# Attention's value products in four column tiles of 32, and another order of the PSUM banks

## The chip, the cores and the metric

The kernel runs on one core of one Trainium2 chip. The metric is device time in microseconds of one execution. The kernel before was timed three times: median 342.35 us, 340.76 to 344.26. The trace is of one further execution. Engines are named as the profile names them: PE multiplies matrices (PEld is its weight load), DVE and ACT work element by element, POOL here mostly issues small transfers, SP issues the large ones.

## What is computed

Attention with a soft cap, then a gated MLP over the sequence, then a gated convolution MLP (batch 2, 12 heads, 448 positions, head size 64):

```python
scores = scale * np.matmul(q, k.transpose(0, 1, 3, 2))
scores = cap * np.tanh(scores / cap)
attn = np.exp(scores - np.max(scores, axis=-1, keepdims=True))
attn = attn / (np.sum(attn, axis=-1, keepdims=True) + 1e-09)
x = np.matmul(attn, v)                      # 12 heads side by side: 448 x 768
h = gelu(x @ w_in);  u, v = halves of h     # the gated MLP
x = x + (u * (w_sg @ layernorm(v) + b_sg)) @ w_out
h = relu(x @ w2_in)                         # the gated convolution
out = (h * sigmoid(conv3(h))) @ w2_out
```

## The kernel before

**Attention, pair by pair.** Twelve pairs of heads N (batch times six) are worked one after the other, both heads of a pair side by side in the 128 partitions. Each pair has two halves. `scores(N, half)` makes transposed scores into a PSUM tile `sc` of four banks, of which there is one copy: half 0 takes key blocks g = 0 and 1 of both heads, half 1 takes block 2 of both and block 3, where the last 64 keys of one head and of the other lie in one tile. These matmuls use split float32r operands and 64-row tiles. ACT then makes tanh of `sc` into `raw` (line 317) and exp of `raw` (line 318). `sc` is written anew by the next half, so the next scores wait for that tanh. For half 0 DVE adds `raw`'s two blocks into `sm` (line 342).

**The values.** `values(N, half)` multiplies `raw` (moving operand, 448 columns, float32) with V (stationary operand) into the bank `pv`, of which there are two, and then sums the exponentials into the bank `su` (one copy) by matmuls with ones: 224 columns, four column tiles of 32 (lines 363 to 372). A float32 matmul stands in the trace as two weight loads and two matmuls. Before, the value products are in two column tiles of 64, one for each head, for g < 3, and in one matmul over all 128 columns for g = 3. All these matmuls are issued by the helper `ordered` and have line 305.

**Order.** The loop of lines 452 to 486 issues a half of scores and then a half of values, one half behind and from R = 13 two halves behind (LAGS). Matmuls of the next stage (`mo`, FILL) stand between them at five places. An attribute keeps PE's order as written; the orders of the other engines are made by a scheduler when the program is built, and each engine works through its own in order.

**What DVE does meanwhile.** It copies `su` to `se` (line 389), so that the next pair's sums may be written; prepares Q and K of later pairs (lines 92, 95, 262, 263); decodes the weights of the next stage from float64 words (lines 135 to 152); and normalises each two pairs: a small transfer `ss` out of `se`, issued on POOL (line 397), a reciprocal (lines 406, 407), two more transfers, a product (line 423) and a split (line 95). The last pair is normalised by PE (`norm_pe`, line 442: `rp`, in a tile of tag `su`; line 446 reads it).

**The next stage.** `rest()` takes seven banks (pool `ps1`) where attention's banks were. Its first unit in that pool is `v_unit` (lines 603 to 605).

Of the kernel before, what the change touches and what calls it, by code (L numbers as in the profile page):

```python
# [9 lines left out]
F32 = mybir.dt.float32  # L10
# [6 lines left out]
P = 128  # L17
B, H, S, D = 2, 12, 448, 64
# [30 lines left out]
def stages(  # L49
# [23 lines left out]
    def pin(last):  # L73
        return tc.issue_after(last[0].ins) if last[0] is not None else ExitStack()
# [12 lines left out]
    def f(ap):  # L87
        return ap.bitcast(F32)
# [130 lines left out]
    def attention(att, psa):  # L219
# [26 lines left out]
        vf = {}  # L246
# [30 lines left out]
        if WARM:  # L277

            wz = att.tile([P, S], F32R, name="wz")
            V.memset(f(wz), 0.0)  # L280
            wps = psa.tile([P, 512], F32, tag="su", name="wps", bufs=1)[:, :S]
            for i in range(WARM):
                T.matmul(wps, lhsT=wz[:, :P], rhs=wz, start=True, stop=True)
        constants(att)
# [17 lines left out]
        def ordered(*args, **kw):  # L302

            with pin(lastm):
                lastm[0] = T.matmul(*args, **kw)  # L305
# [38 lines left out]
        def values(N, half):  # L344
            if half == 0:
                acc[N] = (
                    psa.tile([P, 512], F32, tag="pv", name="pv", bufs=2)[:, :S],
                    psa.tile([P, 512], F32, tag="su", name="su", bufs=1)[:, : S // 2],
                )
            ps, su = acc[N]  # L350
            raw = raws.pop((N, half))
            for g in range(2 * half, 2 * half + 2):
                if g < 3:
                    for h in range(2):
                        r = slice(h * D, (h + 1) * D)
                        ordered(
                            ps[r], lhsT=vf[N][:, g, r], rhs=raw[:, g % 2 * 2 + h],
                            start=g == 0, stop=False, skip_group_check=True,
                        )
                else:  # L360
                    ordered(ps, lhsT=vf[N][:, 3], rhs=raw[:, 2], start=False, stop=True, skip_group_check=True)

            for g in range(2 * half, 3 * half + 1):
                x = raw if half else held.pop(N)
                for t in range(4):
                    h, c = t // 2, (t % 2) * (S // 2)
                    ordered(
                        su[t * 32 : (t + 1) * 32],
                        lhsT=ones[2 if g < 3 else h],
                        rhs=x[:, h if g < 3 else 2, c : c + S // 2],  # L370
                        start=g == 0, stop=g == 3, tile_position=(0, t * 32), skip_group_check=True,
                    )
            if half:
                del acc[N]
                norm(N, ps, su)
# [76 lines left out]
        for R in range(2 * NN + LAGS[1]):  # L452
            N, half = divmod(R, 2)
# [5 lines left out]
            if R < 2 * NN:  # L459
                if half == 0 and N + 2 < NN:  # L460
                    load(N + 2)
                if R == 1:

                    scores(N, half, lambda: values(0, 0))
                    done += 1
                else:
                    scores(N, half)
                if half == 0 and N + 1 < NN:
                    prep_q(N + 1)
                    prep_k(N + 1)  # L470
# [10 lines left out]
            if R - done >= LAGS[R >= LAGS[2]]:  # L481
                values(*divmod(done, 2))
                done += 1
# [414 lines left out]
```

## Time and profile before

| | us |
|---|---|
| median of three runs | 342.35 |
| the profiled execution, whole | 343.89 |
| its span | 342.10 |
| PE busy in the span | 329.2 (96%) |
| DVE busy | 252.9 (74%) |
| ACT busy | 224.9 (66%) |
| attention, first scores to the first `v_unit` | 7.55 to 127.96 |

The profile is of one execution; times are counted from its span's start. A row of the timeline has start, duration, engine, line, operation, tiles written and read, and a count of the instructions merged into it; what stands in brackets is the engine's idle time before it and what ended that. A matmul's start is recorded, its end is modelled, so distances between starts are what is read.

### The profile page before, as it was taken

The numbers are of one execution on the slowest core, as the hardware profiler recorded it, in microseconds if no ns is written. First come the engines' busy times: TensorE is split into PE (matmuls) and PEld (weight loads), VectorE is DVE, ScalarE is ACT, GpSimd is POOL, SyncE is SP. The second block draws the span as 40 slices with busy tenths as digits, with TensorE's granted clock in tenths as the row PEclk, the third lists the DMA queues.
The fourth block names the chain that finished last, engine by engine and source line by source line (L and its number), as shares of the span: only waits on it lengthen the run. The fifth ranks groups of instructions, "written<-read, shape, count | busy, mean of one in ns | idle before, by whom it ended". The sixth has DMA issues, their size and how long they took to land.

```text
span 342.1 us, 5132 instructions
## 1 busy us (share of the span) xinstructions
PE 329.2 (96%) x1814; PEld 252.2 (74%) x1814; DVE 252.9 (74%) x493; ACT 224.9 (66%) x361; POOL 35.8 (10%) x71
## 2 busy tenths in 40 slices
PE   5999999999999999999999999999999999999992
PEld 4544444544456558898899999999999999999991
DVE  3378878889974477997999779997995999970000
ACT  1689988997897246576875554465884988873110
POOL 3000300311034113121111000000000000000000
PEclk9699999999999999999999999999999999999998
DMA  5859555748122114313123383002284113013111
GB/s 174 243 143 278 178 156 158 216 118 218 47 66 63 44 54 148 93 46 94 62 68 119 107 281 150 0 0 62 63 273 158 33 61 92 3 55 126 64 55 34
DMA packets 18698, 37.67 MB, mean 110 GB/s; under 512 B 3980, under 2 KB 9160, under 8 KB 18664
## 3 DMA queue, kind: packets, MB, share of 16 engines
q1 hardware_dynamic: 16952, 34.41, 32.7%
q0 software_dynamic: 1472, 2.61, 2.9%
q8 instruction: 16, 0.26, 0.4%
q10 hardware_dynamic: 240, 0.23, 0.2%
q14 instruction: 18, 0.15, 0.1%
HBM read 34.41 MB, written 2.79 MB: 109 GB/s over the span
## 4 chain that ended last, share of the span: by engine, by line
PE 79%; DMA 7%; DVE 7%; issue 3%; POOL 1%; ACT 0%; SPq 0%; DVEq 0%; ACTq 0%; POOLq 0%
PE mo L98 18%; PE mo L99 17%; PE mo L100 17%; PE pv L305 6%; PE sc L305 5%; PE mo L603 3%; PE mo L604 3%; PE mo L605 3%; PE mo L305 3%; PE su L305 3%; DMA kr<-in_kT_dram 2%; DMA ss<-se 2%; DMA qr<-in_qT_dram 2%; PE idle L305 1%; DVE Q L263 1%
## 5 line engine op out<-in xcount | busy, mean ns | idle before, releaser
L98 PE MATMUL mo<-X,WI 128*128 128x448 f32 x126 | 46.1, 367 | 0.0
L99 PE MATMUL mo<-X,WI 128*128 128x448 f32 x126 | 45.9, 366 | 0.0
L100 PE MATMUL mo<-X,WI 128*128 128x448 f32 x126 | 45.9, 365 | 0.0
L305 PE MATMUL pv<-raw,V 128*64 128x448 f32 (+1 forms) x168 | 43.7, 561 | 0.0
L305 PE MATMUL sc<-Q,K 64*128 64x448 f32 (+1 forms) x252 | 39.7, 398 | 3.4 <-DVE K L92 2.3
L318 ACT ACTIVATE raw<-raw,one 128x1792 f32<-128x1792 f32 (+3 forms) x26 | 39.1, 1503 | 0.6
L305 PEld LDWEIGHTS sc<-Q,K 64*128 64x128 f32 (+1 forms) x252 | 24.8, 190 | 18.0 <-issue 8.1
L130 ACT ACTIVATE f<-f 128x512 f32<-128x512 f32 (+3 forms) x57 | 30.9, 544 | 10.4 <-DMA f<-in_w_out_dram 6.0
L140 DVE SCALAR_TENSOR_TENSOR f<-f 128x512 uint32<-128x512 uint32 (+3 forms) x57 | 30.7, 547 | 9.2 <-ACT f L133 8.7
L317 ACT ACTIVATE raw<-sc 128x1792 f32<-128x1792 f32 (+1 forms) x22 | 32.5, 1475 | 6.8 <-PE sc L305 5.9
L99 PE MATMUL mo<-HG,W 128*128 128x448 f32 x96 | 34.8, 365 | 0.0
L100 PE MATMUL mo<-HG,W 128*128 128x448 f32 x96 | 34.7, 365 | 0.0
L98 PE MATMUL mo<-HG,W 128*128 128x448 f32 x96 | 34.1, 365 | 0.0
L143 DVE SCALAR_TENSOR_TENSOR f<-f 128x512 uint32<-128x512 uint32 (+3 forms) x57 | 30.9, 548 | 0.2
L305 PEld LDWEIGHTS pv<-raw,V 128*64 128x64 f32 (+1 forms) x168 | 11.8, 143 | 21.4 <-issue 18.6
L98 PEld LDWEIGHTS mo<-X,WI 128*128 128x128 f32 x126 | 23.6, 188 | 2.4 <-DVE u L179 0.4
L99 PEld LDWEIGHTS mo<-X,WI 128*128 128x128 f32 x126 | 23.7, 188 | 2.0
L100 PEld LDWEIGHTS mo<-X,WI 128*128 128x128 f32 x126 | 23.6, 188 | 2.0
L783 ACT ACTIVATE o<-mo 128x448 f32<-128x448 f32 x12 | 6.3, 540 | 25.6 <-PE mo L100 22.5
L133 ACT ACTIVATE f<-f 128x256 uint32<-128x256 uint32 (+2 forms) x44 | 22.6, 514 | 0.0
L99 PEld LDWEIGHTS mo<-HG,W 128*128 128x128 f32 x96 | 18.0, 188 | 1.4
L98 PEld LDWEIGHTS mo<-HG,W 128*128 128x128 f32 x96 | 18.0, 188 | 1.4
(141 smaller groups left out, 653.3 us busy)
## 6 DMA issues: line engine op xcount, KB each, us to landing
f<-in_w_in_dram SPq DMA_DIRECT2D x24, 512.0 KB, 4.9
f<-in_w_out_dram SPq DMA_DIRECT2D x24, 256.0 KB, 4.4
V<-in_vL_dram SPq DMA_DIRECT2D x12, 256.0 KB, 4.2
f<-in_w_out_dram SPq DMA_DIRECT2D x8, 384.0 KB, 3.1
qr<-in_qT_dram SPq DMA_DIRECT2D x24, 112.0 KB, 3.2
out_dram<-o SPq DMA_DIRECT2D x12, 224.0 KB, 1.9
rb<-d POOLq DMA_DIRECT2D x22, 112.0 KB, 3.2
kr<-in_kT_dram SPq DMA_DIRECT2D x11, 112.0 KB, 2.6
```

The costliest lines, as they stand in the source:

```text
L98: matmul(ps, lhsT=whi, rhs=xhi, start=start, stop=False)
L99: matmul(ps, lhsT=whi, rhs=xlo, start=False, stop=False)
L100: matmul(ps, lhsT=wlo, rhs=xhi, start=False, stop=stop)
L130: A.activation(f(h), f(h), AF.Copy, scale=2.0**-112)
L133: A.activation(l, l, AF.Copy, scale=0.93 * 2.0**-29)
L140: V.scalar_tensor_tensor(out=l, in0=h, scalar=3, in1=l, op0=ALU.logical_shift_left, op1=ALU.bitwise_or)
L143: V.scalar_tensor_tensor(out=l, in0=h, scalar=0x80000000, in1=l, op0=ALU.bitwise_and, op1=ALU.bitwise_or)
L305: lastm[0] = T.matmul(*args, **kw)
L317: A.activation(raw[:, t], ps[:, t, :S], AF.Tanh, **sc)
L318: lasta[0] = A.activation(raw[:, t], raw[:, t], AF.Exp, scale=capc)
L603: T.matmul(ps, lhsT=xs(0, k), rhs=WI[1][:, 0, k], start=k == 0, stop=False)
L604: T.matmul(ps, lhsT=xs(0, k), rhs=WI[1][:, 1, k], start=False, stop=False)
```

## The change

In `values` every block g is now done in four column tiles of 32, each with its own weight load and its own position, g = 3 too. The moving operand of a tile is still the 448 columns of its head. And the ten warm-up matmuls at the start, whose output is not used, write a tile of tag `sc` rather than `su`. That tag is then the first to be laid out, so that `sc` lies in banks 1 to 4, `pv` in 5 and 6 and `su` in 7, where it was `su` in 1, `sc` in 2 to 5 and `pv` in 6 and 7; the first tile of `ps1` is in bank 1 both times.

```diff
-            wps = psa.tile([P, 512], F32, tag="su", name="wps", bufs=1)[:, :S]
+            wps = psa.tile([P, 4, 512], F32, tag="sc", name="wps", bufs=1)[:, 0, :S]
...
             for g in range(2 * half, 2 * half + 2):
-                if g < 3:
-                    for h in range(2):
-                        r = slice(h * D, (h + 1) * D)
-                        ordered(
-                            ps[r], lhsT=vf[N][:, g, r], rhs=raw[:, g % 2 * 2 + h],
-                            start=g == 0, stop=False, skip_group_check=True,
-                        )
-                else:
-                    ordered(ps, lhsT=vf[N][:, 3], rhs=raw[:, 2], start=False, stop=True, skip_group_check=True)
+                for t in range(4):
+                    r = slice(t * 32, (t + 1) * 32)
+                    ordered(
+                        ps[r], lhsT=vf[N][:, g, r], rhs=raw[:, g % 2 * 2 + t // 2 if g < 3 else 2],
+                        start=g == 0, stop=g == 3, tile_position=(0, t * 32), skip_group_check=True,
+                    )
```

On PE, in the middle of attention, from the scores of one pair's second half on (`K_87` and `K_88` are the two copies of K, `ones_136` to `ones_138` the three tiles of ones):

```order
 L305 MATMUL sc<-Q,K_88 128x448 x9
-L305 MATMUL pv<-raw,V 64x448 x4
+L305 MATMUL pv<-raw,V 32x448 x8
 L305 MATMUL su<-sm,ones_138 32x224 x4
 L305 MATMUL sc<-Q,K_87 128x448 x12
-L305 MATMUL pv<-raw,V 64x448 x2
-L305 MATMUL pv<-raw,V 128x448
+L305 MATMUL pv<-raw,V 32x448 x8
 L305 MATMUL su<-raw,ones_138 32x224 x4
 L305 MATMUL su<-raw,ones_136 32x224 x2
 L305 MATMUL su<-raw,ones_137 32x224 x2
```

Nothing changes its place; seven value matmuls of a pair became sixteen, and value products and sums have one tile shape.

At attention's end on PE, before, with the semaphores waited for (DVE_49 is counted up by DVE, Activation_49 by ACT):

```order
L442 MATMUL rp<-r,sel 64x224 [waits DVE_49,PE_49,Pool_49]
L442 MATMUL rp<-r,sel 64x224 [waits Pool_49]
L442 MATMUL rp<-r,sel 64x224
L442 MATMUL rp<-r,sel 64x224 [waits Pool_49]
L603 MATMUL mo<-WI_77,X 128x512 [waits DVE_49,Activation_49]
```

And the same place now, where lines are three lower:

```order
L439 MATMUL rp<-r,sel 64x224 [waits DVE_49,PE_49,Pool_49]
L439 MATMUL rp<-r,sel 64x224 [waits Pool_49]
L439 MATMUL rp<-r,sel 64x224
L439 MATMUL rp<-r,sel 64x224 [waits Pool_49]
L600 MATMUL mo<-WI_77,X 128x512 [waits DVE_49,Activation_49]
```

Nothing moved, and the first `v_unit` has the waits that it had: in both programs the value that it waits for on DVE is the one set by the product that reads `rp` (line 446, now 443).

On DVE, from the arrival of `ss` to the next copy of `su`, before (`f` are weight pieces in decoding, `WI` where they go):

```order
L406 TENSOR_SCALAR ss<-ss,one 128x14
L135 TENSOR_SCALAR f_530<-f_530 128x512
L423 TENSOR_TENSOR E<-E,rb 128x896
L263 SCALAR_TENSOR_TENSOR Q<-qr,one,Q 128x448
L143 SCALAR_TENSOR_TENSOR f_452<-f_452 128x512
L407 RECIPROCAL ss<-ss 128x14
L149 CAST WI_76<-f_452 128x512
L152 TENSOR_TENSOR WI_76<-f_452,WI_76 128x512
L389 COPY se<-su 128x224
```

And now:

```order
L403 TENSOR_SCALAR ss<-ss,one 128x14
L135 TENSOR_SCALAR f_566<-f_566 128x512
L420 TENSOR_TENSOR E<-E,rb 128x896
L263 SCALAR_TENSOR_TENSOR Q<-qr,one,Q 128x448
L143 SCALAR_TENSOR_TENSOR f_479<-f_479 128x512
L404 RECIPROCAL ss<-ss 128x14
L149 CAST WI_76<-f_479 128x512
L152 TENSOR_TENSOR WI_76<-f_479,WI_76 128x512
L386 COPY se<-su 128x224
```

The order is the same. Over the part of the program that runs, DVE's order differs in one place only, where a weight split (line 152) and a K cast (line 92) that stood next to each other have changed places; the orders of ACT, POOL and SP are the same.

## Rows read from the trace of the kernel before

**Rows 1.** Page, part 1: busy us, share of the span, instructions.

```profile
PE 329.2 (96%) x1814; PEld 252.2 (74%) x1814; DVE 252.9 (74%) x493; ACT 224.9 (66%) x361; POOL 35.8 (10%) x71
```

**Rows 2.** Timeline, PE: values of pair 3, half 0, up to the next scores.

```profile
41.10 0.60 PE L305 MATMUL pv<-raw,V 128*64 128x448 f32 x2
41.53 0.92 PE L305 MATMUL pv<-raw,V 128*64 128x448 f32 x4
42.28 0.55 PE L305 MATMUL pv<-raw,V 128*64 128x448 f32 x2
42.76 0.40 PE L305 MATMUL su<-sm,ones 128*32 128x224 f32 x4
42.97 0.37 PE L305 MATMUL su<-sm,ones 128*32 128x224 f32 x4
43.27 0.47 PE L305 MATMUL sc<-Q,K 64*128 64x448 f32 x2
```

**Rows 3.** Timeline, PE: values of pair 3, half 1, up to the next scores.

```profile
44.69 0.60 PE L305 MATMUL pv<-raw,V 128*64 128x448 f32 x2
45.12 1.12 PE L305 MATMUL pv<-raw,V 128*64 128x448 f32 x3
45.59 1.02 PE L305 MATMUL pv<-raw,V 128*128 128x448 f32 x2
46.07 0.54 PE L305 MATMUL pv<-raw,V 128*128 128x448 f32 x1
46.54 0.40 PE L305 MATMUL su<-raw,ones 128*32 128x224 f32 x4
47.13 0.37 PE L305 MATMUL su<-raw,ones 128*32 128x224 f32 x4
47.43 0.47 PE L305 MATMUL sc<-Q,K 64*128 64x448 f32 x2
```

**Rows 4.** Groups by shape, weight loads of the sums: busy us, mean ns.

```profile
L305 PEld LDWEIGHTS su<-raw,ones 128*32 128x32 f32 x192 | 5.0, 109 | 9.2 <-issue 7.8
```

**Rows 5.** Busy us in stretches: PE, PEld, DVE, ACT, POOL, clock granted, DMA.

```profile
20.84:47.43 26.59, 26.59 (x201) 11.64 (x199) 21.56 (x44) 23.95 (x22) 3.70 (x6) 1.00 0.64 188
53.15:64.23 11.08, 11.08 (x88) 4.87 (x84) 11.01 (x21) 10.73 (x10) 2.94 (x5) 1.00 0.60 179
69.74:87.79 18.05, 17.16 (x124) 8.18 (x123) 17.98 (x34) 15.56 (x15) 2.96 (x5) 1.00 0.60 159
56.72:80.00 23.28, 22.13 (x161) 10.67 (x160) 20.69 (x39) 22.86 (x21) 6.31 (x11) 1.00 0.68 194
90.09:96.21 6.12, 6.12 (x50) 2.50 (x50) 5.69 (x13) 6.08 (x6) 0.50 (x1) 1.00 0.18 47
```

**Rows 6.** Timeline, DVE: copies of su (pairs 3, 5, 7) and arrivals of ss.

```profile
47.57 0.39 DVE L389 COPY se<-su 128x224 f32<-128x224 f32 x1 [0.90 <-PE su L305]
53.15 0.23 DVE L406 TENSOR_SCALAR ss<-ss,one 128x14 f32<-128x14 f32 x1 [1.25 <-DMA ss<-se]
63.84 0.38 DVE L389 COPY se<-su 128x224 f32<-128x224 f32 x1
69.74 0.23 DVE L406 TENSOR_SCALAR ss<-ss,one 128x14 f32<-128x14 f32 x1 [1.95 <-DMA ss<-se]
87.40 0.39 DVE L389 COPY se<-su 128x224 f32<-128x224 f32 x1
```

**Rows 7.** Timeline, PE: sums of pair 7, and the first v_unit.

```profile
78.49 0.38 PE L305 MATMUL su<-sm,ones 128*32 128x224 f32 x2 [0.83 <-DVE se L389]
127.96 0.47 PE L603 MATMUL mo<-WI,X 128*128 128x512 f32 x1 [0.84 <-DVE E L446]
```

**Rows 8.** Timeline, PE and DVE: scores of pair 10, and attention's last handover.

```profile
96.31 0.48 PE L305 MATMUL sc<-Q,K 64*128 64x448 f32 x2
121.49 0.62 DVE L179 SCALAR_TENSOR_TENSOR u<-g,mo 128x448 f32<-128x448 f32 x1 [0.64 <-ACT g L176]
122.29 0.47 PE L98 MATMUL mo<-X,WI 128*128 128x448 f32 x1
```

## The prediction

> **What bounds the kernel now.** I read the page's busy times first: PE is busy in 96% of the span [rows 1], so at first sight whatever PE saves is saved. Then the timeline of PE through one unit of values, to see where time between two matmul starts is more than streaming. Then the busy times of all engines in stretches of attention, because a mean over the span hides that DVE and ACT are full for a part of it [rows 5]. Last the timeline of DVE, to see what its full stretches hang on [rows 6], and the two places where PE waits for DVE [rows 7].
>
> A wave is what I call the matmuls that start within some 20 ns of each other, in different column tiles. In half 0 a wave of two 64-column tiles comes every 0.375 us: 42.28 less 41.53, over two [rows 2]. The first wave takes 0.43, because its weights are not there yet. From the last value wave to the first sum it is 0.48, so 0.105 beyond a wave. A wave of four 32-column tiles, at half the columns, comes every 0.19 (46.54 to 47.13 less a first wave of 0.21, over two), which is half of 0.375 [rows 2, 3]. The last wave of sums to the next scores takes 0.30, 0.11 beyond a wave. In half 1 the change from 64 to 128 columns costs 0.095 (0.47 for a wave), the second weight load of the 128-column tile 0.105 (0.48), the change from 128 to 32 again 0.095 (0.47) [rows 3]. So each change of the tile's shape costs about 0.1 us of PE, and the wider the tile, the more of its first weight load shows.
>
> The whole of half 0's values takes 43.27 less 41.10, 2.17 us, half 1's 47.43 less 44.69, 2.74 us [rows 2, 3]. There are twelve of each.
>
> **What the change does on PE.** Half 0 and half 1 become alike: four waves of values, then two or four of sums, all in one shape. A wave of values with four tiles of 448 columns is not in the trace. Its bounds: 0.375 (twice the 0.19 of four tiles at 224 columns, and also what two tiles take at 448) and 0.75 (if only two of the four ran together). I take 0.375: the sums are the same instruction, float32, 128 rows, four tiles of 32, and differ in the columns alone. First wave: 0.375 and 0.02, as the sums' first is 0.21 against 0.19. From values to sums: between 0 and the present 0.1 beyond a wave; I take 0, since the sums change their moving operand and their weights from g = 2 to g = 3 without a step (the 0.19 above covers it).
>
> Half 0: 0.40 + 3 x 0.375 + 0.19 + 0.30 = 2.015, so 0.155 less. Half 1: 0.40 + 3 x 0.375 + 3 x 0.19 + 0.30 = 2.395, so 0.345 less. A pair saves 0.50 us of PE, twelve pairs 6.0 us. The additional weight loads (32 instead of 14 records for a pair) lie behind running waves, as the sums' do; if that cover were gone, see the third rival.
>
> **The warm-up's tile.** PE's own order keeps warm-up before scores, so the new wait of the first scores costs nothing. At the end, the first v_unit waits 0.84 us for the product that reads rp [rows 7]. Its tile now lies where scores were, not where rp is, but the built program still has the same two waits there, as the order shows. I cost this at 0; the other end is a gain of 0.84.
>
> **How much of 6.0 us arrives.** PE's saving becomes time only where PE is what is waited for.
>
> Up to 47.4 us it is. From 20.84 to 47.43 PE is never idle, DVE is busy 21.56 of 26.59 us and ACT 23.95 [rows 5]. Shortened by three and a half pairs, the stretch is about 24.8 long, so ACT is nearly full but not over. Pairs 0 to 3 lie here: 4 x 0.50 = 2.0 us.
>
> From 47.57 to 87.79 it is not. The copy of pair 3's sums at 47.57 releases the transfer ss, which lands 5.2 us after the copy's end, at 53.15, and DVE sits behind it in its order. Then DVE is busy 11.01 of 11.08 us up to the end of the copy of pair 5's sums. That releases the next transfer, which lands after 5.5 us, at 69.74. Then DVE is busy 17.98 of 18.05 us up to the end of the copy of pair 7's sums at 87.79 [rows 5, 6]. No matmul stands in this chain of 40.2 us; it moves with its start, by 2.0 us, and is no shorter. PE meets it at sm and at su: it already waits 0.83 at pair 7 [rows 7]. What pairs 4 to 7 save, some 2 us, turns into more waiting at those places. ACT is no better: in 56.72 to 80.00 it is idle for 0.42 us [rows 5].
>
> After 87.84 PE leads again, with half 1 of pair 8 and pairs 9 to 11 still to come. Two more places take some back. The scores of pair 10 start at 96.31, and ACT, full since 90.09, ends the tanh they need at 96.2 [rows 5, 8]; that leaves 0.1 of the 0.345 + 0.155 saved just before, and I count 0.05. Then 0.345, 0.155, 0.345 and 0.155 arrive. Of pair 11's last 0.345, the handover keeps all but some 0.1: the matmuls at 122.29 need u, whose last step ends at 121.49 + 0.62 = 122.11 and hangs on matmuls that stand before that half [rows 8]. Sum: 0.05 + 1.00 + 0.1 = 1.15, in all 2.0 + 1.15 = 3.15, say 3.1 us. What comes after moves as a whole, as PE is its bound (96% [rows 1]).
>
> The profiled execution took 343.89 us around a span of 342.10, so 340.8 by its own time. The median of the runs is 342.35, 0.45% below it; the same 3.1 us puts the prediction at **339.2 us**.
>
> **Rivals.**
>
> *The transfers land sooner.* In the chain, ss is slow (5.2 and 5.5 us) when large loads are under way. If the new alignment shortened it, ACT would be the next bound: 2.0, pair 4's 0.50, ACT's 0.42, then 0.35 of pair 7 and the last 1.15, 4.4 us in all: 338.0. Against it: the loads are issued behind the same DVE work and move along with it. If not even ACT held, all of 6.0 us would arrive: 336.3; ACT's 0.42 us of idle time speaks against that.
>
> *The step from values to sums stays.* If the 0.1 belongs to the change of operands and not to the shape, each unit loses 0.1 + 0.02 of its saving: 0.035 and 0.225, a pair 0.26. Four pairs give 1.05, the end about half of 1.15: 1.6 us, 340.7. Against it: between 64 and 128 columns, within one accumulation, the step is as large [rows 3].
>
> *The weight loads come out of cover, and the kernel is slower.* All four tiles use all 128 rows. If a tile's load had to wait for running matmuls of other tiles, each wave would show at least one load of 0.109 us [rows 4]: 4 x 0.109 x 24 = 10.5 us more, less 6.0: 4.5 us slower, 346.8. It decides from 0.063 us in each wave (6.0 over 96 waves), so from waves of 0.44 us. Against it: the sums' waves come at 0.19 with eight loads in 0.38 us [rows 3]. [...]
>
> *The bank order does what it seems meant for.* If the first v_unit no longer waited for rp's reader, 0.84 more: 338.4. The order's waits speak against it.
>
> *Nothing arrives*: the saving is all taken by waits on exp or sm already before 47 us: 342.3.
>
> **Chances.** Forecast 0.55 (its own range 338.4 to 340.0), transfers sooner 0.15, all of it 0.04, step stays 0.14, loads out of cover 0.05, bank order 0.03, nothing 0.04. The range 336.8 to 341.4 takes in the first, second, fourth and sixth with their spread and leaves out under 0.2. About 1% is what a measurement of this kernel can tell from no change. Below 338.9 us lie the second, third and sixth case, and a third of the forecast's own spread: faster 0.40. Slower is the loads' case: 0.05. The rest, 0.55, is within 1%.
>
> **What would show it.** Value waves 0.375 us apart with four matmuls each, and no step from values to sums, so half 0 at 2.0 and half 1 at 2.4 us, up to 47 us at least. Pair 3's copy of su at about 45.6. From there on new PE idle time before su and sm, with DVE as the releaser, of about 2 us more than now; DVE full from the landing of ss to the copy of pair 7's sums, which ends at about 85.8. Scores of pair 10 at about 94.3 behind ACT. The first v_unit at about 124.8, with its wait for DVE as before. I am wrong if the waves are longer than 0.38, if ss lands within 4 us of the copy's end, or if PE's idle time in attention doesn't grow.

## The result, and the profile after

The changed kernel takes 337.68 us (median of 13 runs, 336.82 to 340.33), the kernel before 341.65 beside it (13 runs, 340.76 to 344.26). The ratio is 0.9884, with a 95% interval of 0.9860 to 0.9907: 4.0 us less, between 3.2 and 4.8. The profiled execution of the changed kernel has a span of 335.8 us and 337.68 around it. I forecast a ratio of 0.9908 (339.2 to 342.35), 3.1 us. The time lies within the range, but the number lies nearer to the rival in which the transfers land sooner (338.0).

Lines of the changed kernel stand 3 lower than before (L389 is L386 now, L406 is L403). The page's busy row of the changed kernel, which answers to [rows 1], and its groups of values and their weight loads:

```profile
PE 322.8 (96%) x2030; PEld 252.1 (75%) x2030; DVE 253.1 (75%) x493; ACT 224.6 (67%) x361; POOL 35.0 (10%) x71
L305 PE MATMUL pv<-raw,V 128*32 128x448 f32 x384 | 41.0, 545 | 0.0
L305 PEld LDWEIGHTS pv<-raw,V 128*32 128x32 f32 x384 | 10.1, 109 | 19.1 <-issue 15.2
```

PE is busy 6.4 us less, with 216 matmuls more. Its timeline through half 1 of pair 2 and half 0 of pair 3, which answers to [rows 2, 3] (start, time, matmuls):

```profile
34.26 1.71 PE L305 MATMUL pv<-raw,V 128*32 128x448 f32 x16
35.79 0.94 PE L305 MATMUL su<-raw,ones 128*32 128x224 f32 x16
36.66 1.68 PE L305 MATMUL sc<-Q,K 64*128 64x448 f32 x9
38.32 1.71 PE L305 MATMUL pv<-raw,V 128*32 128x448 f32 x16
39.85 0.56 PE L305 MATMUL su<-sm,ones 128*32 128x224 f32 x8
40.34 1.48 PE L305 MATMUL sc<-Q,K 64*128 64x448 f32 x12
```

Half 0 is now 40.34 less 38.32, 2.02 us (forecast 2.015), half 1 36.66 less 34.26, 2.40 (2.395). The sums start 1.53 after the values: a first wave of 0.40 and three of 0.376, and no step between values and sums. The next scores after half 1 take 1.66 us where they took 1.61.

For the rest I cut attention in three, by starts on PE that every kernel has: **A** from half 1 of pair 0's values to the sums of pair 3's half 1, **B** from there to the sums of pair 8's half 0, **C** from there to the first v_unit. Busy times in these stretches, first of the kernel before, then of the changed one (columns as in [rows 5]):

```profile
20.84:46.54 25.70, 25.70 (x185) 11.22 (x184) 21.43 (x44) 23.16 (x20) 3.70 (x6) 1.00 0.65 190
46.54:87.84 41.30, 40.04 (x294) 19.50 (x293) 35.55 (x67) 37.46 (x34) 7.38 (x12) 1.00 0.61 172
87.84:127.96 40.12, 39.28 (x264) 22.37 (x264) 26.69 (x45) 26.28 (x28) 9.72 (x16) 1.00 0.20 55
```

```profile
19.29:43.28 23.99, 23.99 (x250) 11.55 (x251) 20.56 (x43) 22.79 (x20) 3.85 (x6) 1.00 0.70 203
43.28:82.75 39.47, 38.22 (x377) 19.61 (x369) 36.40 (x68) 37.49 (x34) 7.36 (x12) 1.00 0.61 181
82.75:121.77 39.02, 37.64 (x332) 22.60 (x328) 26.93 (x45) 26.20 (x29) 9.72 (x16) 1.00 0.22 57
```

A is 1.71 us shorter, B 1.83 and C 1.10, together 4.64 between these two executions. I had given B nothing. What follows C is 214.1 us in both. The two starts differ too: A begins at 20.84 before and at 19.29 after. The change accounts for 0.16 of that (pair 0's half 0). The start also moves by some 1 us from execution to execution: A begins at 19.75 in the kernel before run again, and at 20.24 with the new tiles alone.

The chain that I had followed through B, on DVE's timeline of the changed kernel (answers to [rows 6]):

```profile
44.29 0.39 DVE L386 COPY se<-su 128x224 f32<-128x224 f32 x1
48.70 0.23 DVE L403 TENSOR_SCALAR ss<-ss,one 128x14 f32<-128x14 f32 x1
59.92 0.38 DVE L386 COPY se<-su 128x224 f32<-128x224 f32 x1
64.66 0.24 DVE L403 TENSOR_SCALAR ss<-ss,one 128x14 f32<-128x14 f32 x1 [0.68 <-DMA ss<-se]
82.31 0.39 DVE L386 COPY se<-su 128x224 f32<-128x224 f32 x1
```

From the start of the first copy to the end of the last it is 38.41 us, where before it was 40.22. Link by link, before and after: first copy and landing 5.58 and 4.41, DVE to the end of the copy of pair 5's sums 11.08 and 11.60, landing 5.51 and 4.36, DVE to the end of the copy of pair 7's sums 18.05 and 18.04. The last link on DVE is as long as I said; the first is 0.52 longer, 0.33 of it a wait for ACT. The two links with a landing are 2.3 us shorter together. The first of them is no longer set by the landing: DVE comes to L403 without having waited. The profile's own rows of DMA issues, from issue to landing, for the first transfer in the kernel before and in the changed one:

```profile
ss<-se POOLq DMA_DIRECT2D x1, 7.0 KB, 4.9
```

```profile
ss<-se POOLq DMA_DIRECT2D x1, 7.0 KB, 3.2
```

PE's waits over B and C, of the kernel before and of the changed one (us in total, times, longest):

```profile
PE mo L603 <- DVE E L446: 0.8, 1, 0.8
PE su L305 <- DVE se L389: 0.8, 1, 0.8
PE sc L305 <- ACT raw L317: 0.3, 1, 0.3
```

```profile
PE sc L305 <- ACT raw L317: 1.6, 3, 0.7
PE mo L600 <- DVE E L443: 0.8, 1, 0.8
PE mo L98 <- DVE u L179: 0.2, 1, 0.2
```

The forecast said that the waits of sums for DVE would grow by some 2 us. They went away. What came instead are waits of scores for ACT, 1.3 us more: `sc` is not free until ACT has made the tanh (L317). They stand at three places, the first two in B and the third in C:

```profile
62.75 1.48 PE L305 MATMUL sc<-Q,K 64*128 64x448 f32 x12 [0.72 <-ACT raw L317]
74.45 1.69 PE L305 MATMUL sc<-Q,K 64*128 64x448 f32 x9 [0.45 <-ACT raw L317]
91.18 1.28 PE L305 MATMUL sc<-Q,K 64*128 64x448 f32 x7 [0.38 <-ACT raw L317]
```

### The profile page after: what moved, and what is told of

Its sections match the earlier page's. It is cut to its first block, busy times and chain, and to the rows that moved or that the text cites. A ratio compares the mean times of both kernels' runs of the same rounds, so it can differ in the third digit from the quotient of the medians.

```text
span 335.8 us, 5565 instructions
## 1 busy us (share of the span) xinstructions
PE 322.8 (96%) x2030; PEld 252.1 (75%) x2030; DVE 253.1 (75%) x493; ACT 224.6 (67%) x361; POOL 35.0 (10%) x71
## 4 chain that ended last, share of the span: by engine, by line
PE 84%; ACT 9%; DVE 2%; issue 1%; SPq 1%; DMA 1%; DVEq 0%; ACTq 0%
PE mo L98 18%; PE mo L99 18%; PE mo L100 18%; PE sc L305 8%; PE pv L305 6%; ACT raw L317 4%; PE mo L305 3%; PE mo L600 3%; ACT raw L318 3%; PE mo L602 3%; PE mo L601 3%; PE su L305 2%; PE idle L305 1%; ACT f L130 1%; SPq L238 1%
## 5 line engine op out<-in xcount | busy, mean ns | idle before, releaser
L305 PE MATMUL pv<-raw,V 128*32 128x448 f32 x384 | 41.0, 545 | 0.0
L130 ACT ACTIVATE f<-f 128x512 f32<-128x512 f32 (+3 forms) x57 | 31.0, 546 | 10.9 <-DMA f<-in_w_out_dram 6.7
L317 ACT ACTIVATE raw<-sc 128x1792 f32<-128x1792 f32 (+1 forms) x22 | 32.5, 1476 | 3.9 <-PE sc L305 3.4
L305 PEld LDWEIGHTS pv<-raw,V 128*32 128x32 f32 x384 | 10.1, 109 | 19.1 <-issue 15.2
```

What stands on the lines that cost most here:

```text
L130: A.activation(f(h), f(h), AF.Copy, scale=2.0**-112)
L317: A.activation(raw[:, t], ps[:, t, :S], AF.Tanh, **sc)
```

## The experiments

All lengths of A, B and C are read from one profile of each kernel, as the starts in PE's timeline. This table gathers them; "landings" are the times from issue to landing of ss for pairs 3 and 5, and the last two columns are PE's waits in B and C, of sums for DVE (se or sm) and of scores for ACT. "Split" is the splitting of the next stage's weights, which runs on ACT and DVE during attention.

```
kernel                         us      A      B      C    landings  DVE  ACT
before                       341.65  25.70  41.30  40.12  4.9, 5.1  0.8  0.3
before, run again            341.89  25.68  40.32  40.10  4.8, 3.5  0.0  0.3
bank order alone             342.54  25.69  40.75  40.10  4.9, 4.5  0.3  0.3
half 1 as two 64-col tiles   340.82  24.95  40.85  39.55  4.9, 4.6  1.1  0.3
before, no split             349.02  25.69  40.06  40.12  2.3, 2.8  0.0  0.2
changed                      337.68  24.00  39.47  39.02  3.2, 4.0  0.0  1.6
column tiles alone           338.53  24.01  39.34  38.94  4.2, 3.4  0.0  1.8
changed, no split            343.76  24.01  38.00  38.47  2.7, 2.4  0.0  0.2
changed, DVE less            338.36  23.98  39.31  38.91  4.3, 4.4  0.0  1.8
changed, ACT less            341.79  24.72  44.27  38.48  6.7, 2.6  2.9  0.2
changed, low part on POOL    342.21  24.02  42.74  38.97  2.8, 4.6  3.6  0.9
changed, scaling on POOL     346.10  27.66  42.47  38.50  3.9, 3.4  3.9  0.2
before, ss read later        343.36  25.70  40.41  40.56  4.7, 3.6  0.4  0.3
changed, ss read later       342.42  24.79  39.93  40.47  4.9, 3.7  2.0  0.7
```

Times stand beside 342.43 to 342.69 us of the kernel before in these comparisons, and beside 341.65 in the changed kernel's own.

My theory when I began them was that DVE's chain holds B and its landings had come out shorter. The rivals were that PE holds B all along, and that ACT does.

**The bank order alone.** The kernel before, with the warm-up's tile laid where the scores are:

```
-            wps = psa.tile([P, 512], F32, tag="su", name="wps", bufs=1)[:, :S]
+            wps = psa.tile([P, 4, 512], F32, tag="sc", name="wps", bufs=1)[:, 0, :S]
```

> The bank order alone, values as before. Theory A (all of the gain is the tile shape): no change, 0 +- 0.5 us, the first v_unit waits 0.84 us for the reader of rp as before, and value units take 2.17 and 2.74 us. Rival B (the bank order carries part of the 4.0 us): 0.8 us less, with that wait gone; or about 1.5 us less, if the earlier start of the values in the changed kernel's profile (13.95 against 15.66 us) comes from the warm-up's tile.

Measured: 342.54 us against 342.55, ratio 1.0005 (0.9979 to 1.0030). The first v_unit waits 0.8 us for DVE as before. This part of the change does nothing that can be measured.

**The column tiles alone.** The changed kernel with the old line for wps.

> The value tiles alone, banks as before. Theory A: the whole change, 4.0 us less than before (3.2 to 4.8), value units of 2.02 and 2.40 us. Rival B: 2.4 to 3.2 us less, as 0.8 to 1.5 belong to the banks.

Measured: 338.53 us, ratio 0.9901 (0.9868 to 0.9935). The whole gain is the tiles'. Its two landings are 4.2 and 3.4.

**Half 1 as 64-column tiles.** The kernel before, its one 128-column matmul in two:

```
-                    ordered(ps, lhsT=vf[N][:, 3], rhs=raw[:, 2], start=False, stop=True, skip_group_check=True)
+                    for h in range(2):
+                        r = slice(h * D, (h + 1) * D)
+                        ordered(ps[r], lhsT=vf[N][:, 3, r], rhs=raw[:, 2], start=False, stop=True, ...)
```

> Only block g = 3 changes: two tiles of 64 columns instead of one of 128, so that half 1 keeps one shape up to its sums. Theory A (each change of shape costs 0.1 us, a 128-column load 0.1 more): half 1 takes 2.55 instead of 2.74 us, half 0 stays at 2.17, and the step from values to sums stays at 0.10 beyond a wave in both; 12 x 0.19 = 2.3 us of PE, of which 1.3 to 2.3 arrive. Rival C (the step belongs to the change of operands, not of shape): the start of g = 3 still comes 0.47 us after the wave before, half 1 gains only the 0.1 of the load, 1.2 us of PE in all and about 0.7 to 1.2 on the time.

Measured: 340.82 us, ratio 0.9941 (0.9920 to 0.9963). PE's timeline through half 1 of pair 3:

```profile
43.43 1.72 PE L305 MATMUL pv<-raw,V 128*64 128x448 f32 x8
45.08 0.96 PE L305 MATMUL su<-raw,ones 128*32 128x224 f32 x16
45.98 0.47 PE L305 MATMUL sc<-Q,K 64*128 64x448 f32 x2
```

Values take 1.65 us where they took 1.85: the step to 128 columns and its second load are gone. The step to the sums' 32 columns is still there, as 1.65 is 0.43 + 3 x 0.375 + 0.10. With the 32-column tiles it is 1.53, and the step is absent. So the tenth of a microsecond belongs to the change of shape and not to the change of operands. This kernel also shows what I had forecast for B. Its 0.2 us per pair arrive in A (0.74) and in C (0.56), and of the 0.8 that PE saves in B, at landings of 4.9 and 4.6, nothing is seen to arrive: 40.85, where the old tiles at landings of 4.9 and 4.5 gave 40.75. The saving has become waiting for DVE there:

```profile
PE su L305 <- DVE se L393: 1.1, 2, 0.8
```

**The kernel before, once more**, for the spread of the landings.

> The kernel before once more, for a second profile. If the 1.7 us by which the values start earlier in the changed kernel's profile, and the 1.2 us by which each of its two ss transfers lands sooner, are properties of the change, this profile shows the values at 15.6 and DVE waiting some 1.3 and 1.9 us for ss again. If they are chance of one execution, values start between 13.9 and 15.7 and the waits differ from those.

Measured: 341.89 us in one execution. DVE's timeline in B:

```profile
46.47 0.39 DVE L389 COPY se<-su 128x224 f32<-128x224 f32 x1 [0.90 <-PE su L305]
51.97 0.23 DVE L406 TENSOR_SCALAR ss<-ss,one 128x14 f32<-128x14 f32 x1 [1.17 <-DMA ss<-se]
62.68 0.38 DVE L389 COPY se<-su 128x224 f32<-128x224 f32 x1
66.98 0.23 DVE L406 TENSOR_SCALAR ss<-ss,one 128x14 f32<-128x14 f32 x1 [0.29 <-DMA ss<-se]
```

The first landing is as in the execution I had predicted from (5.11 us after the copy's end, 5.19 in that one), the second is not: 3.92, where it was 5.51 [rows 6]. B is 0.98 us shorter for it, and PE does not wait for DVE in it at all. The same program thus has a B of 40.3 or of 41.3. I had built on the longer one. Less PE's wait for DVE (0.83, none and 0.30 us), B is 40.47, 40.32 and 40.45 in the profile of before, in this one and with the bank order alone: that wait is most of what differs.

**Without splitting, before and changed.** Both kernels without the splits of weights in attention; a memset of constants stands for them, so the output is computed with other weights:

```
-                if int(at * 4 + 1) // 2 == R:
-                    wdec(*wi_piece(w_in, j // NK, j % NK), att, 4, hi_eng="v", wait=(3, 4, 5))
+                if j < 2 and R == 1:
+                    G.memset(f(WI[j]), 0.01)
```

> Values as before, but the weight decoding is taken out of attention: no loads of w_in there, none of its work on DVE and ACT; the first stage's weights are a constant instead. Leaves DVE some 38 us and ACT some 8 us less to do in attention. Theory A (DVE, then ACT, hold back part of PE's saving): PE is the bound here all through attention; its waits of 0.83 and 0.19 for the copies of su are gone, so 1 to 2 us less than before. This run is the reference for the next one.

> The changed kernel with the same decoding taken out. Theory A: nothing holds PE back, so it is shorter than the run without decoding before it by nearly all that PE saves: 5.3 to 6.0 us, against 4.0 with the decoding. Rival D (DVE and ACT hold nothing back, the missing third goes elsewhere, after attention or at its end): the difference stays at 3.5 to 4.5 us.

Measured: 349.02 and 343.76 us. Both are slower than their originals for a reason that I had not seen: the memset runs early on POOL, and the first scores come some 6 us later. The first cast of Q on DVE stands beside it. It took 0.40 us in the kernel before; here it takes 7.48 and ends 0.24 after the memset, and the cast of K (L92) that the first scores wait for comes behind it on DVE.

```profile
2.74 10.39 POOL L458 MEMSET WI<- 128x6144 f32 x2
5.89 7.48 DVE L259 CAST Q<-qr 128x448 fp32r<-128x448 f32 x1 [0.51 <-DMA qr<-in_qT_dram]
```

PE waits 9.2 us for K at its start, in both, so they can be compared with each other. The changed kernel is 5.3 us faster. At 0.50 for a pair PE saves 2.13 us in B (four pairs, and 0.13 before pair 8's first sums) and 1.85 in C (three pairs and a half 1). Of that 2.06 and 1.65 now arrive; the 0.2 that C lacks is lost at the handover to u, much as forecast. A remains at 1.68. The landings are 2.3 to 2.8 us here; with the loads of weights and their splits they are 2.6 to 6.7.

**DVE's reading of ss put off.** Two experiments move the operations that read ss, and the transfers behind them, two units later, in the kernel before and in the changed one, so that DVE would not stand waiting for the landing:

```
-            later(3, s1)
-            later(4, s1b)
+            k = 3 if last else 5
+            later(k, s1)
+            later(k + 1, s1b)
```

> The kernel before with the same later reciprocal. Theory A: PE led almost everywhere before, so only its 1.0 us of waiting for copies of su can go: 0 to 1.0 us less than before, and less than the changed kernel gains by it or about as much. Rival E: no change.

> The changed kernel with the reciprocal and the next transfers of each normalisation but the last one half later, so that DVE has other work while ss is on its way. Theory A: DVE no longer waits for ss (0.7 to 3 us in attention); 0.3 to 1.2 us less than the changed kernel, since ACT is full in the same stretch. Rival E (ACT alone holds, DVE's wait for ss is covered): the same time as the changed kernel within 0.3 us.

Measured: 343.36 us (ratio 1.0020, 0.9997 to 1.0043) and 342.42 (0.9976, 0.9944 to 1.0007). The ratios are to the kernel before. The first shows no difference. The second is slower than the changed kernel, whose ratio is 0.9884, and misses both expectations: the reciprocals now come back late, and DVE waits for them in front of the product that the next steps need.

```profile
DVE E L420 <- DMA rb<-d: 6.7, 3, 3.0
```

PE waits 2.0 us for se in consequence and 1.8 instead of 0.8 before the first v_unit. What was to free DVE has only put the wait one transfer further on. This explains B and C (0.5 and 1.5 us longer than in the changed kernel). Of the 5.3 us by which this profile is longer, 3.1 lie earlier, before DVE's later reading can count: PE stood 2.15 us for sm before 16.15, and the granted clock was 0.50 from 16.42 to 23.25 us. As a test of who holds B it says little.

**A step of the split on POOL.** The changed kernel, with the subtraction for the low part (L152) on POOL instead of DVE; and, apart from it, the scaling of the high words (L130) on POOL instead of ACT:

```
-            V.tensor_tensor(out=lo, in0=f(l), in1=f(hi), op=ALU.subtract)
+            G.tensor_tensor(out=lo, in0=f(l), in1=f(hi), op=ALU.subtract)
```

```
-                A.activation(f(h), f(h), AF.Copy, scale=2.0**-112)
+                G.tensor_scalar(out=f(h), in0=f(h), scalar1=2.0**-112, scalar2=None, op0=ALU.mult)
```

> The changed kernel, with one step of the weights' splitting in attention, the subtraction that leaves the low part (12 pieces of about 0.69 us, 8.3 us in all), taken from DVE and given to POOL. The question is what holds the changed kernel between the end of pair 3's scores and the sums of half 1 (the stretch of 39.4 us, 38.0 with no splitting at all): If DVE's queue of splits and reciprocals holds it, the stretch comes down by 0.7 to 1.4 us and the kernel to about 336.5 to 337 us against 337.7. If ACT's loop of exponentials holds it, or PE alone, nothing: 337.4 to 338. Rival: POOL, which also issues the transfers of the sums and reciprocals, runs the subtraction for longer than DVE and they leave later: the stretch grows by 1 to 2 us and the kernel stands at 339 to 340.

> The changed kernel, with another step of the same splitting, the scaling of the high words (12 pieces of about 0.67 us, 8 us in all), taken from ACT and given to POOL. If ACT's loop holds the stretch from pair 3's scores to the sums of half 1, it comes down by about 1 us (the 0.42 us by which the scores of pairs 9 and 10 wait for ACT, and the 0.04 per pair), the kernel to about 336.7. If DVE's queue holds it, nothing, 337.4 to 338. Rival: POOL takes 1.5 us or more for a piece, the splits on DVE behind it start later, and the kernel is 1 to 2 us slower, 339 to 340.

Measured: 342.21 us (ratio 0.9998, 0.9974 to 1.0022) and 346.10 (1.0109, 1.0081 to 1.0138): slower, as the rival said in both, but by more than its 1 to 2 us (339 to 340). B is 3.3 and 3.0 us longer, with waits for DVE before the sums. In the second A is 3.7 longer too: PE waited 1.44 and 0.42 us for ACT, and the granted clock was 0.50 from 27.17 to 30.57 us. POOL takes 1.50 and 2.13 us for a piece. In the first, that is not the worst of it. One piece on POOL, and two operations on DVE beside such pieces:

```profile
70.44 1.63 POOL L152 TENSOR_TENSOR WI<-f,WI 128x512 fp32r<-128x512 f32 x1
```

```profile
45.97 1.95 DVE L342 TENSOR_TENSOR sm<-raw 128x896 f32<-128x896 f32 x1
70.79 1.56 DVE L92 CAST K<-kr 128x512 fp32r<-128x512 f32 x1
```

They take 1.09 and 0.42 us where POOL is idle (so at 45.78 and 46.79 us in the changed kernel). The operation on `sm` began 0.32 us after POOL's piece of 45.65 us, is 0.86 longer, and that piece ran on for 1.00 after its start. The cast begins 0.35 us after POOL's piece and ends 0.28 after its end: it is longer by 1.14 us, and the piece ran on for 1.28 after its start. The cast beside the memset, above, is 7.08 us longer, with the memset running on for 7.24. Why the operations on DVE are longer there is not shown. In both of these experiments some of DVE's operations were longer than in the changed kernel: the one on `sm` took 1.26 us on average in the first, against 1.09, and the subtraction for the low part 0.71 in the second, against 0.69.

**DVE less and ACT less.** Two steps left out and given to no one, each in the changed kernel: on DVE the step that puts in the sign, on ACT the scaling (both 12 pieces, some 8 us). The output is computed with other weights in both.

```
+            if sign:
                 V.scalar_tensor_tensor(
                     out=l, in0=h, scalar=0x80000000, in1=l, op0=ALU.bitwise_and, op1=ALU.bitwise_or
                 )
```

```
+                if scale:
                     A.activation(f(h), f(h), AF.Copy, scale=2.0**-112)
...
-                out=l, in0=h, scalar=3, in1=l, op0=ALU.logical_shift_left, op1=ALU.bitwise_or
+                out=l, in0=h, scalar=3 if scale else 2, in1=l,
+                op0=ALU.logical_shift_left if scale else ALU.logical_shift_right, op1=ALU.bitwise_or
```

> The changed kernel, with one step of the weights' splitting in attention left out and given to no one: the one that puts the sign into the assembled word (DVE, 12 pieces of 0.69 us, 8.3 us in all, eight of them between the end of pair 3's scores and the sums of half 1). The output is then computed with weights that have lost their sign; no other operation changes. That stretch is 39.47 us in the changed kernel and 38.00 without any splitting, the one after it (to the output's first product) 39.02 and 38.47. If DVE's queue holds the changed kernel there: 38.0 to 38.6 us and 38.5 to 38.7, the kernel 1 to 2 us under 337.7, 335.7 to 336.7. If ACT's loop holds it: 39.2 to 39.5 and 39.0, the kernel 337.2 to 337.9.

> The changed kernel, with another step of the same splitting left out: the scaling of the high words (ACT, 12 pieces of 0.67 us, 8 us in all); the shift behind it on DVE then goes the other way, at the same length, so that the words stay small. The output is computed with other weights; no other operation changes. If ACT's loop of exponentials holds the changed kernel between pair 3's scores and the sums of half 1, that stretch falls from 39.47 us to 38.0 to 38.6, the two waits of the scores for ACT there (0.40 and 0.42 us) and the 0.04 per pair go, and the kernel stands at 335.7 to 336.7. If DVE's queue holds it: 39.0 to 39.5 us, and the kernel 337.0 to 337.9.

Measured, DVE less: 338.36 us (ratio 0.9889, 0.9860 to 0.9917, where the changed kernel has 0.9884), B 39.31 and C 38.91. Eight microseconds off DVE change nothing, and DVE now waits for ACT. Its waits, the largest first, and PE's in B and C:

```profile
DVE sm L343 <- ACT raw L319: 9.7, 9, 2.5
```

```profile
PE sc L306 <- ACT raw L318: 1.8, 3, 0.7
```

So at landings of 4.3 and 4.4 us, with 8 us less on DVE, B is no shorter: DVE's chain no longer holds the changed kernel there, and my theory for it has fallen.

Measured, ACT less: 341.79 us (338.76 to 345.02; ratio 0.9940, 0.9905 to 0.9975), which neither theory had. The profile shows two different things. C is 38.48, as without any split (38.47), and 38.50 with the scaling on POOL. So it is ACT that costs the changed kernel some 0.5 us in C, where the scores of pair 10 wait for the tanh. B is 44.27, and it begins with the first landing. DVE's timeline and PE's wait:

```profile
45.34 0.39 DVE L388 COPY se<-su 128x224 f32<-128x224 f32 x1
52.73 0.23 DVE L405 TENSOR_SCALAR ss<-ss,one 128x14 f32<-128x14 f32 x1 [3.49 <-DMA ss<-se]
57.43 0.38 DVE L388 COPY se<-su 128x224 f32<-128x224 f32 x1
```

```profile
PE su L307 <- DVE sm L344: 2.9, 1, 2.9
```

Behind that wait, PE's next values and sums, and the stretch around them (columns as in [rows 5]):

```profile
62.40 3.10 PE L307 MATMUL pv<-raw,V 128*32 128x448 f32 x16
65.33 0.93 PE L307 MATMUL su<-raw,ones 128*32 128x224 f32 x16
```

```profile
58.44:65.27 6.83, 6.31 (x36) 2.83 (x40) 6.08 (x11) 1.66 (x1) 1.92 (x4) 0.50 0.93 226
```

The transfer took 6.7 us from issue to landing, DVE stood still for 3.49 of them, and PE's sums of the next half waited 2.9. This is the mechanism of my prediction, with a size that I had not thought of. And more was lost than the wait: within the 2.89 us in which PE stood the granted clock went to 0.50, and it stayed there for 6.83 us; that the one brought on the other is not shown. From the values' start to the sums' it was 2.93 us where it is 1.53. Half of 6.83, some 3.4 us, is an estimate of what the clock took, from the granted 0.50 and these two times. B less the wait and less this is 38.0, as long as without any split. A is 0.72 longer as well; PE waited 0.62 us for ACT there. That the landing was as long in the other runs of this kernel is not shown; their spread of 6 us fits it.

ACT holds the changed kernel in B as in C. PE's three waits for ACT stand in three stretches from one start of values to the next: from pair 5's half 1 (first stretch) and pair 7's half 0 (second), both in B, and from pair 9's half 0 (third), in C:

```
kernel                      first  second  third
changed                      7.44    5.65   5.31
column tiles alone           7.43    5.66   5.32
changed, DVE less            7.41    5.66   5.32
changed, no split            6.89    4.86   4.86
changed, ACT less            8.28    4.85   4.86
changed, scaling on POOL     6.89    6.88   4.86
```

Less work on DVE changes none of the three. With the scaling off ACT the second and the third are as long as without any split (the first lies partly in the stretch with a clock of 0.50 there, and the 6.88 holds a wait of 1.83 us for DVE). In B the changed kernel's surplus over the kernel without the split is 1.47 us, and the first two stretches hold 0.55 and 0.79 of it. For the first stretch alone the proof is weaker: in the run with 6.89, PE had stood 1.07 us for DVE shortly before, in which ACT could catch up.

No kernel of these was faster than the changed one.

## Why the prediction was right, and where it was not

**The waves, the steps and the units: right.** 0.376 us for a wave of four, no step to the sums, half 0 at 2.02 and half 1 at 2.40. The rival with the loads out of cover is out: four loads of 109 ns stand in each wave of 0.376, with none of it added, and the waves are no longer than those of two tiles (0.375). The rival in which the step stays is out by the same rows, and the 64-column experiment says why.

**The bank order at nothing: right**, by the experiment with it alone.

**A at 2.0 (in the stretch that can be compared, three pairs and the values of one half 1, 1.50 + 0.32): nearly.** It gave 1.70. The term that was too large is the pair: 0.46 arrives and not 0.50. The scores that follow half 1 are 0.04 longer (1.66 against 1.61). ACT's timeline of the changed kernel, beside them:

```profile
34.38 1.67 ACT L317 ACTIVATE raw<-sc 128x1792 f32<-128x1792 f32 x1 [0.19 <-PE sc L305]
36.04 0.55 ACT L387 ACTIVATE E<-pv 128x448 f32<-128x448 f32 x1
36.48 1.79 ACT L318 ACTIVATE raw<-raw,one 128x1792 f32<-128x1792 f32 x1
```

From the first operation, which waits for the scores, to the end of the last, at 38.27, ACT has no gap, and the next values start at 38.32, right behind it. Before, the copy still waited 0.18 for PE, and the values began 0.18 after the last one's end. PE's part has become shorter than ACT's by 0.04 there. The term is the same with the scaling or the whole split left out (1.655 to 1.660), so it comes from these three operations and not from the split.

**B at nothing: the step that failed.** The prediction put it so: "No matmul stands in this chain of 40.2 us; it moves with its start, by 2.0 us, and is no shorter." Of DVE's own links the last was as long as I took it (18.04 for 18.05) and the other 11.60 for 11.08, but the landings between them are no constants. I read 5.2 and 5.5 us from one execution; the same program gave 5.1 and 3.9 in the next, and B fell from 41.30 to 40.32. With three profiles of the old tiles B is 40.79 on average, with two of the new ones 39.41: 1.4 us arrived, a rough figure, as the three differ by 1.0. The medians of 13 runs give some 1.0 for B, if A (1.7), C (1.1) and pair 0's half 0 (0.16) are taken off 4.0; their interval, 3.2 to 4.8, leaves 0.2 to 1.8. Above the kernels without the split (40.06 and 38.00), the old tiles lose 0.7, about half of it to DVE's chain (0.83, none and 0.30 in the three), and the new ones 1.4, nearly all of it to ACT. So B keeps back about a third of the 2.06 that PE saves there, and not all.

There was a sign of it in my own rows. PE waited 0.83 us for this chain in the whole stretch [rows 7]. A chain that lets PE idle for 0.83 in 41.3 lies close to PE's own time, and I priced it as if it alone set the length. If its landings come 1 us sooner, PE's time is what counts again. I had that case as a rival, at 4.4 us and a chance of 0.15; A, B and C gave 1.7, 1.4 and 1.1, 4.2 in all, and ACT was the next bound as that rival had it (1.27 for B). The half-1 experiment shows the forecast's own case, where the landings stay and B gives nothing. Which of the two came went with the landings in these profiles; no run set a landing by itself.

**What the chain gives way to: right in kind.** In the rival I had ACT as the next bound, with 0.42 us of idle time to give. After the change PE waits 1.3 us more for ACT in B and C, relief of DVE brings nothing, and without ACT's scaling the stretches at pair 7 and pair 9 are 0.80 and 0.45 us shorter.

**C at 1.15: right**, 1.10 between the first two profiles and 1.13 between the means of three and two. Scores of pair 10 waited for ACT's tanh as said (they start at 91.18 behind 0.38 us), the first v_unit kept its wait of 0.84, and the handover at u took 0.2.

**The forecast's list of disproofs** had "ss lands within 4 us of the copy's end" and "PE's idle time in attention doesn't grow". The first came true for one of the two transfers (it was issued 0.3 us after the copy's end and landed 3.2 later; the other took 4.36). The second did not: PE's idle time over A, B and C went from 2.10 us to 2.63. But it grew elsewhere than I had said: before sums, where I had looked for 2 us more behind DVE, it went away, and it came back before scores, behind ACT. The time stayed in the range because A and C carried two thirds of it, and because the range reached to the rival's price; as far as B goes, that was luck.

**What stays open:** why the first landing is 4.7 to 4.9 us in all five profiles with the old tiles in half 0 and the whole split, and 2.8 to 6.7 with the new ones. A load of the weights (512 KB) is issued in the same few us, between 47 and 54 us in the kernel before and between 44 and 50 in the changed one, and a change of pace may move the two against each other, but no run here set that distance by itself.

## What to carry to other kernels

A chain through a transfer is as long as the transfer's landing in that execution (5.51 us and 3.92 from the copy's end for the same one here): before it is called a bound, look at the landing in a second profile, and at how long the bounded engine really stands idle behind it, for that idle time was most of what the chain added here (0.83 of 41.3 us). One wait of 2.89 us came with 6.83 us at a granted clock of 0.50, an estimated 3.4 us more. Price a saving in such a stretch between "nothing" and "all of it", ask which engine is the next to hold it (here ACT), and give both ends weight. When a shape of matmul tiles changes from one unit to the next, look for the step at the seam (0.1 us here); one shape throughout saved it here, even with 216 matmuls more.

## What the runs showed of the hardware

A transfer of 7 KB took 2.3 to 2.8 us from issue to landing without the weights' loads and splits, 3.2 to 5.1 in the kernel before and the changed one, and 6.7 once (pairs 3 and 5); in one and the same program the second of two was 5.1 in one execution and 3.5 in another. An operation on DVE of 0.42 us took 1.56 beside a subtraction on POOL, and one of 0.40 took 7.48 beside two memsets of 10.39 in all. In one run a wait of 2.89 us on PE came with 6.83 us at a granted clock of 0.50, which took some 3.4 us more by the estimate above. And with 216 matmuls more, and their loads, PE was busy 6.4 us less: a wave of four tiles of 32 columns took 0.376 us, one of two of 64 columns 0.375.
